# Two float32 products in place of split float16 ones, in an attention chain with a written-out order

## The chip, the cores and the metric

The kernel runs on one core of a Trainium2 chip. The metric is the device time of one execution in microseconds; lower is better.

## The reference

Three layers run one after the other: a gated delta-rule attention over 768 steps for 4 batches and 8 heads of 48 columns, a layer of 8 experts of which each token takes one, and a feed-forward layer.

```python
k_n = k / (np.linalg.norm(k, axis=-1, keepdims=True) + 1e-06)
state = np.zeros((B, H, D, D), dtype=np.float32)          # B, H, D = 4, 8, 48
for t in range(S):                                        # S = 768
    kt, vt, bt = (k_n[:, :, t], v[:, :, t], beta[:, :, t, None])
    y[:, :, t] = np.einsum('bhd,bhde->bhe', q[:, :, t], state)
    v_old = np.einsum('bhde,bhd->bhe', state, kt)
    state = state + bt[:, :, :, None] * np.einsum('bhd,bhe->bhde', kt, vt - v_old)
...
logits = x @ w_gate; expert_idx = np.argmax(logits, axis=1)
out[mask] = gate_w[mask, None] * (np.maximum(xe @ w1[e], 0.0) @ w2[e])   # for each expert e
...
h = x @ w_in
return ((h * (1.0 / (1.0 + np.exp(-h)))) @ w_out).astype(np.float32)
```

## The kernel before, in words

The 768 steps are cut into 6 chunks of 128. A *group* is one chunk of one batch with all 8 heads, 24 groups in all; two batches make a *pair*, 12 pairs, and the state of a batch goes from one chunk to the next, which is two pairs or four groups later. For a group the kernel does:

- load k, q and v (`lk`, `lq`, `lv`, DMAs on SP's queue), normalise k and q (`kn`, `nrm...`), and split each into a float16 high and low part (`knh`, `knl` into the tile `TMk`; `qh`, `ql`), transpose them by DMA (`trk`, `trq`), and copy rows of the transposed k to `KX` by three DMAs (`kx`);
- the Gram matrices: L is K K' under a mask, P is K Q' under a mask. `mm0` to `mm3` write a bank of PSUM each, `mt0` to `mt3` multiply it by the mask on VectorE, `mh...` takes the float16 high part on ScalarE, `ml...` the low part on GpSimd. A bank holds two heads, each with L and P side by side;
- invert the triangular matrix: its 16x16 diagonal blocks go through a scratch in DRAM (`scr`, `lm`), are inverted on VectorE and GpSimd with one block on each partition (`l0` to `lo`), and come back (`st`, `tv`) as the tile `TV`; three levels of products double the blocks (`xm`, `xe`, `Tm`, `Te`, `Vm`, `Ve` with 16, 32 and 64);
- the chain: `rm` multiplies the state (two float16 parts in `Ss`) by K, `re` and `rh` form the right side, `z0m` and `z0h` apply the inverse, `em` and `ee` form the residual with both parts of L, `zm` corrects. The result Z is split in two (`zh` on ScalarE, `zl` on VectorE). `sm` adds K'Z to the state (three float16 products for each head), `se`, `sh` and `sl` store it and its two parts in partitions 0 to 47 of `Ss`, and `sd` copies them to partitions 64 to 111, so that one product takes both parts of k or q. `ym` forms P Z (three products for each head) and adds the state's part; `ye` scales it;
- the router's part: transpose (`rt`), logits in float32 (`rl`, line 900), and the places of the tokens.

The class `Plan` writes the order of all these steps once for every engine and for SP's queue, by a table of steps with durations and needs (`GROUP`, `PAIR`), a table of which buffers are held from which step to which (`GHELD`, `PHELD`), and a table of shifts (`LATER`); on the chip each engine then works off its own queue in that order. The experts and the feed-forward part follow; no step of theirs is touched.

Lines of the profile: 529 is `mm`, 533 `mt`, 538 `mh`, 543 `ml`; 722 is the state's product in `rm` and `ym`; 773 `zh`, 777 `zl`; 784 to 786 `sm`; 798 `sl`; 801 `sd`; 807 to 809 `ym`; 552 `scr`, 557 `tv`, 473 `kx`, 645 the larger products of the block inversion.

Of the kernel before, what the change touches and what calls it, by code (L numbers as in the profile page):

```python
# [24 lines left out]
ISC = 1.0 / SC  # L25
# [3 lines left out]
class Plan:  # L29
# [17 lines left out]

    GHELD = """k lk / sqk kn; q lq / sqq ql; s2 sqk / sqr; s2 sqq / sqq; s2 vq / vq; kn kn / knl; TTk trk / rm mm0 mm1 mm2 mm3; TTq trq / ym mm0 mm1 mm2 mm3; KX kx / mm0 mm1 mm2 mm3;
        t mt0 / ml0; t mt1 / ml1; t mt2 / ml2; t mt3 / ml3; Mh mh0 mh1 mh2 mh3 / ym; Ml ml0 ml1 ml2 ml3 / ym; TV tv / zm; Rh rh / zm; Z0h z0h / zm; Z0s zs / em; Zh zh / sm ym;
        Zl zl / sm ym; xT rc / rl; pm mm0 / mt0; pm mm1 / mt1; pm mm2 / mt2; pm mm3 / mt3; pi xm16 / xe16; pi Tm16 / Te16; pi Vm16 / Ve16; pi xm32 / xe32; pi Tm32 / Te32;  # L50
        pi Vm32 / Ve32; pi xm64 / xe64; pi Vm64 / Ve64; pc rm / re; pc em / ee; pc sm / se; pc ym / ye; pz z0m / z0h; pz zm / zl; pr rt / rc; pr rl / rg"""
# [7 lines left out]
    LAND = dict(lk=3.4, lq=2.8, lv=2.7, trk=2.8, trq=2.7, kx=2.2, scr=2., lm=5., st=5., tv=4., rs=4.)  # L59
    START = dict(P=0.5, A=1, V=0.7, G=0.7, D=1.75)  # L60
    EARLY, LOOK = 14.40, 0.00
    LATER = dict(
        l42=226, ql=9, ee=-190, l22=198, vp=14, rt=61, Vm16=98, zl=-42, z0m=-172, ml1=4, l40=10, Te32=6, xm16=-111, z0h=-6, mm2=75, vr=-7, rb1=160,
        rb3=-152, mh2=-84, xe16=-29, nrm2=210, ym=13, xm32=-49, mm3=10, Tm32=-146, rp=-89, l21=6, em=-44, mt2=-48, mt0=-4, xe32=-7, trk=6, Vm64=-19,
        knl=-120, bl0=-42, l8c=-30, Ve64=-12, zt1=-2, nrs=-81, sh=-3, sm=-90, zx64=59, se=-20, l8b=2, l43=-4, b1=29, b3=-52, zs2=10, lo=-8, l0p=-34,
        nrm1=15, sd=51, zs0=20, kn=-25, zxo=10, l23=-124, zt7=16, nrm0=-18, Te16=30, l0=7, rb=2, lm=-6, vu1=-23, zk0=-30, b2=-14, nrm7=6)
    SLOW = 1.4

    def __init__(self, chunks, pairs, bufs, held, scratch, setup):
# [36 lines left out]
        for s in ("knh", "knl"):  # L106
            for r in ("sm", "trk"):
                after(s, r, held)
# [151 lines left out]
class Attention:  # L260
# [6 lines left out]
    BUFS = dict(k=3, q=3, v=3, ss=2, r0=1, r1=1, w=5, rn=2, s2=1, kn=1, TTk=6, TTq=8, KX=2, t=3, Mh=8, Ml=8, Lm=2, Ln=1, Tl=2, pr=1, Xl=1, TVl=1, TV=3,  # L267
                Rh=2, Z0h=2, Z0s=2, Zh=2, Zl=2, ysc=2, m1=2, m2=2, vsc=6)
    TMK, NSCR = 8, 2
# [22 lines left out]
    def constants(self):  # L292
# [4 lines left out]
        self.TMk = [cp.tile([128, 8, 128], F16, name=f"TMk{i}") for i in range(self.TMK)]  # L297
        self.TMq = cp.tile([128, 8, 128], F16, name="TMq")
# [13 lines left out]
    def setup(self):  # L312
# [18 lines left out]
        z = self.wk.tile([128, 1, 1028], F16, tag="Ml", name="zeros16", bufs=self.BUFS["Ml"])  # L331
# [4 lines left out]
        for i, t in enumerate(self.Ss):  # L336
            add(f"zs{i}", "G", 0.4, [], [(i, "sh")], zero(t))
# [77 lines left out]
    def front(self, pi, g, c, b, a, pr):  # L415
# [3 lines left out]
        TMk = self.TMk[g % self.TMK]  # L419
# [34 lines left out]
        def kn():  # L454
            st["kn"] = self.sb([H, D], F32, "kn")
            nc.gpsimd.tensor_tensor(out=st["kn"], in0=st["k"], in1=self.bc(pr["rn"][:, a, 0:8], D), op=ALU.mult)
# [7 lines left out]
        def knh():  # L464
            nc.scalar.activation(out=self.part(TMk, False), in_=st["kn"], func=AF.Copy)

        def knl():
            nc.gpsimd.tensor_tensor(out=self.part(TMk, True), in0=st["kn"], in1=self.part(TMk, False), op=ALU.subtract)
# [44 lines left out]
    def bank(self, i):  # L513

        return slice(2 * i, 2 * i + 2)

    def grams(self, pi, g, c, b, a, pr):
# [3 lines left out]
        out = []  # L521
        for i in range(4):
            def mm(i=i):
                mp = st["mp", i] = self.pm.tile([128, 2, 256], F32, tag="pm", name="mp")
# [10 lines left out]
            def mh(i=i):  # L535
                if "Mh" not in st:
                    st["Mh"] = self.sb([H, 256], F16, "Mh")
# [170 lines left out]
    def chain(self, pi, g, c, b, a, pr):  # L708
# [91 lines left out]
        def sd():  # L800
            nc.vector.tensor_copy(Ss[64:112], Ss[0:48])
# [561 lines left out]
```

## Time and profile before

| | us |
|---|---|
| median of 3 runs (lowest, highest) | 1137.92 (1135.22, 1139.65) |
| the profiled execution's own time | 1134.98 |
| its span, first to last instruction | 1133.2 |

| engine | busy in the span | share |
|---|---|---|
| TensorE (PE) | 932.6 us | 82% |
| VectorE (DVE) | 671.9 us | 59% |
| ScalarE (ACT) | 539.0 us | 48% |
| GpSimd (POOL) | 368.3 us | 33% |

The shares are means over two different parts. In the first 440 us, the attention with the router, the engines share the work and none is full; after that TensorE works nearly without a break. The page's clock row (PEclk) gives the granted TensorE clock in tenths of the full one: 6 to 9 in the first part, 9 in the second. A busy time of an engine is the time covered by its instructions, and an instruction that stands behind something after it began counts as busy.

### The profile page before, as it was taken

How to read it: one execution, taken by the hardware profiler on the slowest of the kernel's cores; microseconds unless marked ns; L12 is line 12 of the kernel's file. 1: busy time of each engine (PE TensorE's matmuls, PEld its weight loads, DVE VectorE, ACT ScalarE, POOL GpSimd, SP SyncE). 2: the span in 40 equal slices, each digit the busy share in tenths (PEclk: the TensorE clock that was granted, in tenths of full speed). 3: DMA queues.
4: the chain of work that ended last, by engine and by line, in shares of the span. 5: the costliest groups of instructions: out<-in, count | busy, mean ns of one | idle time of the engine just before them, and what ended most of it. 6: DMA issues, size and time to landing. Idle time of an engine off the chain costs nothing. (4 is left out here: it accounts for less than half of the span.)

```text
span 1133.2 us, 21329 instructions
## 1 busy us (share of the span) xinstructions
PE 932.6 (82%) x8404; PEld 843.4 (74%) x8405; DVE 671.9 (59%) x1371; ACT 539.0 (48%) x1094; POOL 368.3 (33%) x353
## 2 busy tenths in 40 slices
PE   0437766676777874589999999999999999999995
PEld 0436666575666763579899999899999999999995
DVE  5797888988798843544444469974333343433332
ACT  4547767676767673434333344643233233323321
POOL 5866555756566312553233320001001010100101
PEclk9657767868678796699999999999999999999998
DMA  8885766857677523643344444520000000000000
GB/s 227 178 168 105 164 142 124 186 106 151 132 149 114 102 54 104 188 133 115 114 136 136 136 150 130 154 70 28 1 1 28 1 29 1 15 15 1 28 1 31
DMA packets 223667, 108.96 MB, mean 96 GB/s; under 512 B 164296, under 2 KB 210120, under 8 KB 223560
## 3 DMA queue, kind: packets, MB, share of 16 engines
q1 hardware_dynamic: 219208, 97.37, 36.6%
q0 software_dynamic: 4352, 10.16, 2.9%
q8 instruction: 68, 1.11, 0.5%
q14 instruction: 39, 0.32, 0.2%
HBM read 71.34 MB, written 16.50 MB: 78 GB/s over the span
## 5 line engine op out<-in xcount | busy, mean ns | idle before, releaser
L1099 PE MATMUL po<-w,g 128*128 128x384 f32 x1152 | 218.4, 338 | 0.0
L1099 PE MATMUL pf<-yb,w 128*128 128x512 f32 x864 | 216.6, 395 | 1.0 <-ACT yb L1174 0.5
L1099 PEld LDWEIGHTS po<-w,g 128*128 128x128 f32 x1152 | 204.7, 188 | 9.0 <-ACT g L1189 0.4
L1099 PEld LDWEIGHTS pf<-yb,w 128*128 128x128 f32 x864 | 161.2, 188 | 31.4 <-DVE yb L1175 0.9
L1216 POOL DMA_INDIRECT out_dram<-ob,idsi x24 | 25.0, 1043 | 440.4 <-DVE ob L1215 434.9
L1187 DVE TENSOR_TENSOR sg<-pf,sg 128x512 f32<-128x512 f32 x96 | 66.2, 690 | 171.8 <-ACT sg L1186 171.7
L1186 ACT ACTIVATE sg<-pf 128x512 f32<-128x512 f32 x96 | 57.4, 598 | 194.1 <-PE pf L1099 193.4
L543 POOL TENSOR_TENSOR Ml<-t,Mh 128x512 f16<-128x512 f32 x96 | 113.4, 1194 | 59.6 <-ACT Mh L538 58.2
L1099 PE MATMUL py<-h,w 128*128 128x432 f32 x576 | 127.7, 362 | 5.3 <-ACT yT L1139 3.4
L1099 PE MATMUL ph<-xT,w 128*128 128x432 f32 x576 | 125.7, 363 | 1.0 <-DVE xT L1071 1.0
L1099 PEld LDWEIGHTS py<-h,w 128*128 128x128 f32 x576 | 106.1, 188 | 13.5 <-DVE h L1122 4.4
L1099 PEld LDWEIGHTS ph<-xT,w 128*128 128x128 f32 x576 | 110.1, 191 | 6.5 <-DVE xT L1071 1.3
L529 PEld LDWEIGHTS <-KX 112*128 112x128 f16 x768 | 67.7, 127 | 52.8 <-issue 32.0
L529 PE MATMUL mp<-TTk,KX 112*128 112x128 f16 x384 | 67.7, 273 | 47.6 <-DVE t L533 29.2
L1190 DVE TENSOR_TENSOR g<-sg,g 128x512 fp32r<-128x512 f32 x96 | 66.3, 691 | 55.1 <-PE po L1099 41.8
L1189 ACT ACTIVATE g<-sg 128x512 fp32r<-128x512 f32 x96 | 60.6, 631 | 62.6 <-DVE sg L1187 62.5
L1045 DVE TENSOR_TENSOR w<-raw,w 128x768 fp32r<-128x768 f32 (+1 forms) x56 | 60.6, 1093 | 30.4 <-ACT w L1044 30.1
L538 ACT ACTIVATE Mh<-t 128x512 f16<-128x512 f32 x96 | 59.4, 625 | 39.6 <-DVE t L533 38.9
L533 DVE TENSOR_TENSOR t<-mp,c 128x512 f32<-128x512 f32 x96 | 64.8, 682 | 17.1 <-PE mp L529 15.4
L1121 ACT ACTIVATE h<-ph 128x432 fp32r<-128x432 f32 x64 | 33.6, 524 | 76.6 <-PE ph L1099 74.8
L1044 ACT ACTIVATE w<-raw 128x768 fp32r<-128x768 f32 (+1 forms) x56 | 51.6, 934 | 33.7 <-DMA raw<-in_moe_w_dram 33.6
L529 PE MATMUL mp<-TTq,KX 112*128 112x128 f16 x384 | 67.5, 276 | 0.0
(189 smaller groups left out, 1750.8 us busy)
## 6 DMA issues: line engine op xcount, KB each, us to landing
TV<-scr SPq DMA_DIRECT2D x24, 512.0 KB, 4.5
raw<-in_moe_w_dram SPq DMA_DIRECT2D x24, 512.0 KB, 4.3
raw<-in_moe_w_dram SPq DMA_DIRECT2D x32, 384.0 KB, 4.0
KX<-TTk SPq DMA_DIRECT2D x72, 96.0 KB, 3.3
raw<-in_moe_w_in_dram SPq DMA_DIRECT2D x12, 512.0 KB, 4.9
raw<-in_moe_w_out_dram SPq DMA_DIRECT2D x16, 384.0 KB, 3.1
xd<-x SPq DMA_DIRECT2D x12, 392.0 KB
k<-in_k_dram SPq DMA_DIRECT2D x24, 192.0 KB, 2.8
```

What stands on the lines that cost most here:

```text
L529: nc.tensor.matmul(mp[:, j, o:o + 128], KX[0:112, x, u], st[t][0:112, u], start=x == 0, stop=x == 1)
L533: nc.vector.tensor_tensor(out=t, in0=st["mp", i], in1=self.con.mask.to_broadcast([128, 2, 256]), op=ALU.mult)
L538: nc.scalar.activation(out=st["Mh"][:, self.bank(i)], in_=st["t", i], func=AF.Copy)
L543: nc.gpsimd.tensor_tensor(out=st["Ml"][:, self.bank(i)], in0=st["t", i], in1=st["Mh"][:, self.bank(i)], op=ALU.subtract)
L1044: nc.scalar.activation(out=h, in_=x, func=AF.Copy)
L1045: (nc.gpsimd if slow else nc.vector).tensor_tensor(out=l, in0=x, in1=h, op=ALU.subtract)
L1099: self.nc.tensor.matmul(out, a, b, start=first and i == 0, stop=last and i == n - 1)
L1121: nc.scalar.activation(out=h[:, 0, 0:W], in_=ph[:, 0:W], func=AF.Relu)
L1186: nc.scalar.activation(out=gf, in_=ph, func=AF.Sigmoid)
L1187: nc.vector.tensor_tensor(out=gf, in0=ph, in1=gf, op=ALU.mult)
L1189: nc.scalar.activation(out=g[:, 0], in_=gf, func=AF.Copy)
L1190: nc.vector.tensor_tensor(out=g[:, 1], in0=gf, in1=g[:, 0], op=ALU.subtract)
```

## The change

The products P Z and K'Z become float32: Z is kept as one float32 tile, P as the masked float32 tile `Pt`, and K as the normalised float32 tile `KN` (8 fixed ones instead of one in turn). So `zl` goes, and only L has a high and a low part: `mh` and `ml` are two for a group, not four. A Gram bank now holds four heads of L (`mm0`, `mm1`, which need only `kx`) or four heads of P (`mm2`, `mm3`, which also need the transposed q). The state's copy `sd` becomes a DMA on SP's queue. The buffers change: `Mh` and `Ml` from 8 of 256 columns a head to 5 of 128, `Pt` 6, `TMk` from 8 to 3. The tables of durations, buffers and shifts of `Plan` change with it, and so the written order on all engines.

```diff
-        mt0 V .6 mm0; ... mh0 A .52 mt0; mh1 A .52 mt1; mh2 A .52 mt2; mh3 A .52 mt3; ml0 G 1.11 mh0; ...
+        mt0 V .6 mm0; ... mh0 A .55 mt0; mh1 A .55 mt1; ml0 G 1.11 mh0; ml1 G 1.11 mh1;
...
-    EARLY, LOOK = 14.40, 0.00
+    EARLY, LOOK = 19.26, 0.00
...
-        l42=226, ql=9, ee=-190, l22=198, vp=14, rt=61, Vm16=98, zl=-42, z0m=-172, ml1=4, ...
+        l42=193, vp=14, Vm16=98, zl=-42, ml1=17, l40=-105, Te32=6, xm16=-26, z0h=-6, ...
-    SLOW = 1.4
+    SLOW = 1.2
...
-                for j, u in enumerate(range(H)[self.bank(i)]):
-                    for o, t in ((0, "TTk"), (128, "TTq")):
-                        for x in range(2):
-                            nc.tensor.matmul(mp[:, j, o:o + 128], KX[0:112, x, u], st[t][0:112, u], start=x == 0, stop=x == 1)
+                for j, u in enumerate(range(H)[s]):
+                    for x in range(2):
+                        nc.tensor.matmul(mp[:, j], KX[0:112, x, u], st[t][0:112, u], start=x == 0, stop=x == 1)
...
-            st["Zh"] = self.sb([H, D], F16, "Zh")
+            st["Zh"] = self.sb([H, D], F32, "Zh")
             nc.scalar.activation(out=st["Zh"], in_=st["zq"], func=AF.Copy, scale=ISC)
-
-        def zl():
-            st["Zl"] = self.sb([H, D], F16, "Zl")
-            nc.vector.scalar_tensor_tensor(out=st["Zl"], in0=st["zq"], scalar=ISC, in1=st["Zh"], op0=ALU.mult, op1=ALU.subtract)
...
             for u in range(H):
-                h, l = (TMk[:, u, r:r + 48] for r in (0, 64))
-                nc.tensor.matmul(sp[:, u], h, Zh[:, u], start=True, stop=False)
-                nc.tensor.matmul(sp[:, u], l, Zh[:, u], start=False, stop=False)
-                nc.tensor.matmul(sp[:, u], h, Zl[:, u], start=False, stop=True)
+                nc.tensor.matmul(sp[:, u], KN[:, u], st["Zh"][:, u], start=True, stop=True)
...
         def sd():
-            nc.vector.tensor_copy(Ss[64:112], Ss[0:48])
+            nc.sync.dma_start(Ss[64:112], Ss[0:48])
...
             for u in range(H):
-                h, l = st["Mh"][:, u, 128:256], st["Ml"][:, u, 128:256]
-                nc.tensor.matmul(yp[:, u], h, st["Zl"][:, u], start=True, stop=False)
-                nc.tensor.matmul(yp[:, u], h, st["Zh"][:, u], start=False, stop=False)
-                nc.tensor.matmul(yp[:, u], l, st["Zh"][:, u], start=False, stop=c == 0)
+                nc.tensor.matmul(yp[:, u], st["Pt"][:, u], st["Zh"][:, u], start=True, stop=c == 0)
                 if c > 0:
                     state(yp[:, u], ("TTq", u), False)
```

On TensorE, at a head of P Z (`pc` is the bank of PSUM, `Ss` the state, `TTq` the transposed q), before:

```order
L807 LDWEIGHTS Mh
L807 MATMUL pc<-Zl,Mh 128x48
L808 LDWEIGHTS Mh
L808 MATMUL pc<-Zh,Mh 128x48
L809 LDWEIGHTS Ml
L809 MATMUL pc<-Zh,Ml 128x48
L722 LDWEIGHTS TTq
L722 MATMUL pc<-Ss_128,TTq 128x48
L722 LDWEIGHTS TTq
L722 MATMUL pc<-Ss_128,TTq 128x48
```

and now, with two heads:

```order
L811 MATMUL pc<-Zh,Pt 128x48
L736 LDWEIGHTS TTq
L736 MATMUL pc<-Ss_131,TTq 128x48
L736 LDWEIGHTS TTq
L736 MATMUL pc<-Ss_131,TTq 128x48
L811 MATMUL pc<-Zh,Pt 128x48
```

The three pairs of weights and product are one float32 product, whose weights have no row of their own here; the state's two products stay between them.

On VectorE, in the middle of the attention part, from one right side (`v`) through the state's low part (`Ss<-Sm`) to the state's copy, before:

```order
L777 SCALAR_TENSOR_TENSOR Zl<-pz,Zh 128x384
L732 SCALAR_TENSOR_TENSOR v<-v,vsc,pc 128x384
L437 TENSOR_REDUCE ss<-s_4397 128x8
L792 SCALAR_TENSOR_TENSOR Sm_125<-pc,vsc,Sm_125 48x384
L509 TENSOR_SCALAR ysc<-w,vsc 128x2
L798 SCALAR_TENSOR_TENSOR Ss_129<-Sm_125,vsc,Ss_129 48x384
L533 TENSOR_TENSOR t<-mp,c_71 128x512 x2
L751 TENSOR_TENSOR Z0s<-Z0h,sign 128x384
L533 TENSOR_TENSOR t<-mp,c_71 128x512
L581 TENSOR_SCALAR Ln<-Lm 128x256
L801 COPY Ss_129<-Ss_129 48x768
```

and now:

```order
L746 SCALAR_TENSOR_TENSOR v<-v,vsc,pc 128x384
L542 TENSOR_TENSOR Lt<-mp,c_71 128x512 x2
L765 TENSOR_TENSOR Z0s<-Z0h,sign 128x384
L797 SCALAR_TENSOR_TENSOR Sm_127<-pc,vsc,Sm_127 48x384
L776 SCALAR_TENSOR_TENSOR Rh<-pc,v 128x384
L803 SCALAR_TENSOR_TENSOR Ss_131<-Sm_127,vsc,Ss_131 48x384
L542 TENSOR_TENSOR Pt<-mp,c_71 128x512
L689 TENSOR_TENSOR X_119<-lv,c_71 128x32x16
L746 SCALAR_TENSOR_TENSOR v<-v,vsc,pc 128x384
```

The low part of Z and the copy have no row any more; the masked copies write `Lt` twice, then `Pt`.

On SP's queue, where the first chunk's states are stored, before:

```order
L638 DMA scr_104<-TVl 128x16x16 x2
L477 DMA_TRANSPOSE TTq<-TMq 128x8x128
L428 DMA k<-in_k_dram 128x384
L428 DMA v<-in_v_dram 128x384 x2
L473 DMA KX_114<-TTk 48x1024 x3
L552 DMA scrM<-Mh 64x8x64 x2
L477 DMA_TRANSPOSE TTq<-TMq 128x8x128
L557 DMA TV<-scr_104 128x8x256
```

and now:

```order
L434 DMA v<-in_v_dram 128x384
L806 DMA Ss_131<-Ss_131 48x768
L434 DMA v<-in_v_dram 128x384
L566 DMA scrM<-Mh 64x8x64 x2
L434 DMA k<-in_k_dram 128x384
L482 DMA_TRANSPOSE TTk<-TMk_105 128x8x128
L434 DMA q<-in_q_dram 128x384
L482 DMA_TRANSPOSE TTq<-TMq 128x8x128
L478 DMA KX_117<-TTk 48x1024 x3
L806 DMA Ss_132<-Ss_132 48x768
```

The state's copy (`Ss`) stands among the loads, the scratch write and the transposes of other groups.

## Rows read from the trace of the kernel before

**Rows 1.** Busy time by stretch (us, instructions), then granted clock, DMA share, GB/s

```profile
core 0: us, PE busy (x) PEld busy (x) DVE busy (x) ACT busy (x) POOL busy (x), PEclk, DMA share, GB/s
0.00:60.00 60.00, 16.03 (x134) 13.95 (x135) 39.87 (x97) 31.86 (x76) 40.41 (x63) 0.81 0.87 204
60.00:360.00 300.00, 205.20 (x3686) 182.04 (x3687) 257.44 (x597) 204.01 (x478) 188.87 (x184) 0.74 0.72 141
360.00:440.00 80.00, 63.43 (x1316) 55.58 (x1314) 48.07 (x132) 52.05 (x120) 20.28 (x18) 0.81 0.33 72
440.00:1133.00 693.00, 647.97 (x3269) 591.82 (x3269) 326.52 (x549) 251.04 (x422) 118.74 (x89) 0.97 0.23 70
```

**Rows 2.** Groups of DVE, 0 to 440 us: busy us, mean ns | idle before

```profile
L533 DVE TENSOR_TENSOR t<-mp,c 128x512 f32<-128x512 f32 x96 | 64.8, 682 | 17.1 <-PE mp L529 15.4 <-POOL Ml L543 0.8 <-POOL v L446 0.6
L798 DVE SCALAR_TENSOR_TENSOR Ss<-Sm,vsc,Ss 48x384 f16<-48x384 f32 x20 | 22.0, 1098 | 0.8 <-ACT Ss L795 0.8
...
L801 DVE COPY Ss<-Ss 48x768 f16<-48x768 f16 x20 | 18.8, 942 | 0.6
...
L777 DVE SCALAR_TENSOR_TENSOR Zl<-pz,Zh 128x384 f16<-128x384 f32 x24 | 13.2, 550 | 7.1 <-ACT Zh L773 7.0
...
L501 DVE TENSOR_TENSOR r<-r,r 128x18 f32<-128x18 f32 x12 | 7.2, 604 | 0.2
```

**Rows 3.** Single lines of DVE: shortest, median and longest ns

```profile
L801 DVE COPY Ss<-Ss x20: 353/386/3153, 114.9 to 408.7; 48x768 f16<-48x768 f16 x20
...
L798 DVE SCALAR_TENSOR_TENSOR Ss<-Sm,vsc,Ss x20: 598/604/3656, 113.5 to 407.6; 48x384 f16<-48x384 f32 x20
...
L501 DVE TENSOR_TENSOR r<-r,r x12: 156/178/1950, 15.6 to 309.6; 128x18 f32<-128x18 f32 x12
```

**Rows 4.** Timeline near 246 us, DVE and POOL: start us, duration us

```profile
246.28 1.52 POOL L645 TENSOR_TENSOR pr<-Tl,Xl 128x512 f32<-128x512 f32 x1
246.60 2.52 DVE L801 COPY Ss<-Ss 48x768 f16<-48x768 f16 x1
...
247.75 1.16 POOL L543 TENSOR_TENSOR Ml<-t,Mh 128x512 f16<-128x512 f32 x1
```

**Rows 5.** The page's costliest groups: low and high parts of the Gram banks

```profile
L543 POOL TENSOR_TENSOR Ml<-t,Mh 128x512 f16<-128x512 f32 x96 | 113.4, 1194 | 59.6 <-ACT Mh L538 58.2
...
L538 ACT ACTIVATE Mh<-t 128x512 f16<-128x512 f32 x96 | 59.4, 625 | 39.6 <-DVE t L533 38.9
```

**Rows 6.** Groups of PE, 60 to 360 us: the first product of P Z

```profile
L807 PE MATMUL pc<-Zl,Mh 128*128 128x48 f16 x128 | 19.2, 199 | 1.8 <-DVE v L732 1.4 <-DVE Sm L792 0.4
```

**Rows 7.** Timeline of PE, four places: P Z twice, the logits twice

```profile
239.82 0.21 PE L807 MATMUL pc<-Zl,Mh 128*128 128x48 f16 x1
239.86 0.21 PE L808 MATMUL pc<-Zh,Mh 128*128 128x48 f16 x1
...
434.80 0.18 PE L808 MATMUL pc<-Zh,Mh 128*128 128x48 f16 x1
434.83 0.18 PE L809 MATMUL pc<-Zh,Ml 128*128 128x48 f16 x1
...
245.42 0.81 PE L900 MATMUL ps<-wg,xT 128*128 128x8 f32 x6
246.10 0.35 PE L688 MATMUL lv<-X,TV 128*128 128x32 f16 x8
...
264.01 1.45 PE L900 MATMUL ps<-wg,xT 128*128 128x8 f32 x6 [0.83 <-ACT xT L895]
265.31 0.48 PE L767 MATMUL pz<-Z0h,c 128*128 128x384 f16 x1
```

**Rows 8.** DMA issues: count, KB each, median us to landing

```profile
KX<-TTk SPq DMA_DIRECT2D x72, 96.0 KB, 3.3
```

**Rows 9.** Waits of SP's queue, 0 to 436 us: total us, times, longest

```profile
SPq L557 <- PE pz L769: 23.6, 4, 8.5
```

**Rows 10.** Waits of all engines, 60 to 420 us: total us, times, longest

```profile
PE pc L786 <- DVE Zl L777: 9.4, 9, 2.8
```

More of the change, by code (lines that the diff above doesn't have):

```diff
@@ L106, in __init__ @@
         for s in ("knh", "knl"):
-            for r in ("sm", "trk"):
-                after(s, r, held)
+            after(s, "trk", held)
+        for s in ("knl", "sm"):
+            after("kn", s, normed)
         for s in ("rm", "ym"):
@@ L297, in constants @@
         self.TMk = [cp.tile([128, 8, 128], F16, name=f"TMk{i}") for i in range(self.TMK)]
+        self.KN = [cp.tile([128, 8, 48], F32, name=f"KN{i}") for i in range(self.NKN)]
         self.TMq = cp.tile([128, 8, 128], F16, name="TMq")
@@ L324, in setup @@
             add(n, "G", 0.15, [], u, zero(t.rearrange("p u (r c) -> p (u r) c", r=2)[:, :, 48:64]))
+        for i, t in enumerate(self.Ss):
+            add(f"zs{i}", "G", 0.4, [], [(i, "sh")], zero(t))
         for i, t in enumerate(self.KX):
@@ L464, in knh @@
         def knh():
-            nc.scalar.activation(out=self.part(TMk, False), in_=st["kn"], func=AF.Copy)
+            nc.scalar.activation(out=self.part(TMk, False), in_=KN, func=AF.Copy)
         def knl():
-            nc.gpsimd.tensor_tensor(out=self.part(TMk, True), in0=st["kn"], in1=self.part(TMk, False), op=ALU.subtract)
+            nc.gpsimd.tensor_tensor(out=self.part(TMk, True), in0=KN, in1=self.part(TMk, False), op=ALU.subtract)
         def kx():
@@ L511, in norms, with four @@
         return [("nrs", nrs), *self.steps("nrm", nrm), ("ysc", ysc)]
-    def bank(self, i):
-        return slice(2 * i, 2 * i + 2)
+    def four(self, i):
+        return slice(4 * i, 4 * i + 4)
     def grams(self, pi, g, c, b, a, pr):
@@ L536, in mh, with ml @@
+            out += [(f"mm{i}", mm), (f"mt{i}", mt)]
+        for i in range(2):
+            s = self.four(i)
+            def mh(s=s):
                 if "Mh" not in st:
-                    st["Mh"] = self.sb([H, 256], F16, "Mh")
-                nc.scalar.activation(out=st["Mh"][:, self.bank(i)], in_=st["t", i], func=AF.Copy)
-            def ml(i=i):
+                    st["Mh"] = self.sb([H, 128], F16, "Mh")
+                nc.scalar.activation(out=st["Mh"][:, s], in_=st["Lt"][:, s], func=AF.Copy)
+            def ml(s=s):
@@ L541, in ml @@
                 if "Ml" not in st:
-                    st["Ml"] = self.sb([H, 256], F16, "Ml")
-                nc.gpsimd.tensor_tensor(out=st["Ml"][:, self.bank(i)], in0=st["t", i], in1=st["Mh"][:, self.bank(i)], op=ALU.subtract)
-            out += [(f"mm{i}", mm), (f"mt{i}", mt), (f"mh{i}", mh), (f"ml{i}", ml)]
+                    st["Ml"] = self.sb([H, 128], F16, "Ml")
+                nc.gpsimd.tensor_tensor(out=st["Ml"][:, s], in0=st["Lt"][:, s], in1=st["Mh"][:, s], op=ALU.subtract)
+            out += [(f"mh{i}", mh), (f"ml{i}", ml)]
@@ L667, in xm @@
                 for u in range(H):
-                    nc.tensor.matmul(xp[:, u], st["Mh"][:, u, 0:128], Ta[:, u], start=m != 16 or u == 0, stop=m != 16)
+                    nc.tensor.matmul(xp[:, u], st["Mh"][:, u], Ta[:, u], start=m != 16 or u == 0, stop=m != 16)
                 if m == 16:
```

86 lines of the change are left out of this document (43 added, 43 removed).

## The prediction

> **What bounds the kernel now.** I read the table of stretches first [rows 1]. The program is two programs in a row: the attention part with the router until about 440 us, and the experts and the feed-forward part after it. The diff touches only the first, so its 440 us are what can change. In the long middle of it, 60 to 360 us, no engine is full: VectorE (DVE) is busy 257.4 of 300 us, TensorE (PE) 205.2, ScalarE (ACT) 204.0, GpSimd (POOL) 188.9, and the DMA engines have a busy share of 0.72. TensorE's granted clock is 0.74 there, so it changes between its two levels of 1.2 and 2.4 GHz. The engine nearest to full is DVE, at 86%; the missing 14% are waits on other engines in queues of fixed order. That is why I treat DVE as what sets the pace, with a rate of 300/257.4 = 1.17 us of time for each us of the busiest engine.
>
> Then I read what DVE spends its time on [rows 2], and the shortest, median and longest time of its forms [rows 3]. The copy of the state (L801) has a median of 386 ns and a mean of 942; the low part of the state (L798) 604 and 1098; a tiny 128x18 sum (L501) 178 and 604. In the order of time one sees why [rows 4]: the copy that began at 246.60 ended at 249.12, while POOL ran two tensor operations back to back from 246.28 to 248.91. DVE's busy time thus holds time in which it only stood behind POOL.
>
> **The change part by part.**
>
> *VectorE.* The low part of Z (L777, 24 x 550 ns = 13.2 us) and the copy of the state (L801, 18.8 us) go: 32.0 us [rows 2]. The masked copies of the Gram banks (L533) stay 96 of 128x512. The waits behind POOL shrink too. In L798 they are 20 x (1098 - 604) = 9.9 us, in L501 12 x (604 - 178) = 5.1 [rows 2, 3]. POOL loses half of its 113.4 us of low parts of the Gram matrices [rows 5], 56.7 of the 40.4 + 188.9 + 20.3 = 249.6 us it is busy up to 440 us [rows 1], so 23%. I take 23% of these 15 us, 3 us; the bounds are nothing and all 15, since I cannot tell which POOL instruction caught which DVE one. Sum for DVE: -35 us of 345.4 [rows 1], three quarters of it in the middle stretch (257.4/345.4), -26: it falls from 257 to 231 us.
>
> The Trainium skill (SBUF — State Buffer, "SBUF: two separate sides") says that DVE and GpSimd share one pair of ports as an exclusive lock, held for a whole instruction, against a DVE operation in a two-port mode or with two SBUF inputs. The long copy agrees [rows 4]; by that rule the copy's 11 us of waiting go whole (they are in the 18.8 already), and what is left falls with POOL's share, as above.
>
> *ScalarE and GpSimd.* Half of the high parts (L538, 48 x 625 ns = 30 us) and half of the low parts (L543, 48 x 1194 ns = 57 us) go [rows 5]. Neither engine is the fullest, so I give their time nothing by itself; it shortens the queues in which others' work stands.
>
> *TensorE.* Here the change costs. P Z took 24 float16 products of 48 columns for a group (8 heads x 3), each with its own weights; they follow each other every 40 ns where the clock is low and every 25 to 30 where it is high [rows 7]. Now it is 8 float32 products. The trace has one float32 product with weights of 128x128 already, the router's logits (L900): three products show as six instructions, and the next work begins 0.68 us after them at the high level (245.42 to 246.10) and 1.30 us after at the low one (264.01 to 265.31) [rows 7]. That is 0.113 and 0.217 us for an instruction. Eight products are 16 such: 1.8 us at the high level, 3.5 at the low one, against 24 x 0.025 = 0.6 and 24 x 0.040 = 0.96 before. They move 48 columns where the logits move 8; if that does not hide behind the loading of weights it adds at most two float16 steps of 40 ns to each, 16 x 0.297 = 4.8 us. So P Z costs +1.2 to +3.8 us for a group. With a mean clock of 0.74, about half of the time is at each level, so 16 x 0.167 = 2.7 against 0.8: +1.9.
>
> K'Z goes from 24 products to 8 in float32 with weights of 48 columns. No row shows those weights. Below, they keep the float16 pace: 16 x 0.040 = 0.64 for 24 x 0.040 = 0.96, a gain of 0.3 us. Above, they cost as much as the logits: 2.7 for 0.8, +1.9. I take +0.5, nearer to the float16 end because the weights are three eighths as wide. L807, the first of P Z's products, stands 128 times in the middle stretch, 8 for a group: 16 groups [rows 6]. TensorE then has 205 + 16 x (1.9 + 0.5) = 243 us there; the bounds are 205 + 16 x 0.9 = 219 and 205 + 16 x 5.7 = 296.
>
> The Trainium skill (TensorE: Matmul & The Clock Gate, "Weight-path perf modes — Fast Weight Load (FWL) and DoubleRow") speaks against the change: quick loading of weights is on for 128 columns of a type that is not FP32, so float32 weights lose it. The trace agrees as far as it goes: 40 ns for a float16 step, 217 for a float32 one at the same level [rows 7]. By the page's P / 1.2 ns, 107 ns for a load of 128 columns, P Z would be 16 x 0.107 = 1.7 us, an estimate that the rows outdo.
>
> *The DMA.* The second copy of the state becomes 20 transfers on SP's queue, each behind the low part of the state (L798) of its batch, so each can hold up what follows it there. In the row of the new order, loads of v, k and q and the transposes stand behind it; those feed groups that come later. The nearest row is the copy of K' rows (KX, also 48 partitions): 3.3 us to landing [rows 8]. The copy is wanted one chunk later, four groups on; at 300/16 = 19 us a group for the middle that is over 50 us. So its landing is hidden. If the queue is late, the cost is that of the waits below, in the third rival.
>
> *The order of the Gram banks.* At the start the banks of L of groups 0 and 1 now come before any bank of P. The scratch write of L of the first pair waits for two masked copies and two high parts for a group, not four: 2 x 682 + 2 x 625 ns = 2.6 us for a group, 5 for the pair [rows 2, 5]. POOL, busy 40.4 of the first 60 us, has less in front too [rows 1]. I take -6 us for the start, between 0 and -12. In the last stretch, 360 to 440 us, PE is busy 63.4 of 80 us and DVE only 48.1 [rows 1], so there the longer P Z counts: the groups end one behind the other, and of +1.9 - 0.55 us for each of the last few about 3 us stay, between 0 and +8.
>
> **Sum.** The fullest engine of the middle goes from DVE's 257 us to PE's 243 (DVE 231): 14 us less, at 1.17 us each -16. With -6 at the start and +3 at the end: -19 us. The profiled execution, from which all durations are, took 1134.98 us (span 1133.2), so 1116 by its own time; the median of the runs shown is 1137.92, 3 us more, and so 1119 us.
>
> **The rivals.**
>
> *VectorE keeps the pace (faster still).* If TensorE's work packs tighter and the high clock holds, PE has 219 us, DVE all of the relief behind POOL: 257 - (32 + 15) x 0.75 = 222. Then 222 x 1.17 = 259, -41 in the middle, -6 at the start: 1091 us. For it: PE waits 9.4 us in K'Z for the low part of Z alone, and that goes [rows 10]. Against it: DVE and PE would then be equally full, and queues of fixed order wait for both.
>
> *TensorE becomes the bound (slower).* The float32 products run at the low level, and the columns do not hide: P Z 4.8 - 0.96 = +3.8 us, K'Z +0.7, together +4.5. PE has 205 + 72 = 277 us, at 1.17 that is 324: +24 in the middle, +5 at the end, 1167 us. It decides from 52/16 = 3.3 us for a group upwards, where PE reaches the 257 us that DVE has now. For it: the granted clock of 0.74, and that half of the logits shown ran at the low level [rows 1, 7]. Against it: the logits' step includes their own moving columns, and PE now has 95 idle us in the stretch to take work into.
>
> *The queue of SP holds the pace (no change).* SP's queue already stands for 23.6 us, in four places, with the load of the inverses (L557) behind a product of TensorE [rows 9]. Twenty more transfers, each stuck behind DVE for a us or two, are 20 to 40 us of the queue; the loads behind come later by as much, and the relief of the engines becomes idle time: 1138, within 6. Against it: the scratch write gets half of its wait removed, and the loads run one or more groups ahead.
>
> **How the numbers follow.** A difference of 0.5%, 5.7 us, is about what a measurement of this kernel can tell from none. The forecast has a chance of 0.47, VectorE's pace 0.22, TensorE as the bound 0.17, SP's queue 0.14. Faster: nearly all of the first, all of the second and a third of the last: 0.70. Slower: nearly all of the third rival but one, a little of the last: 0.16. Same: 0.14. For 8 in 10 the range goes from the fast rival, 1091, to 1148, which leaves out the dear half of the slow one. The forecast's own range is 1103 to 1132.
>
> **What would show it.** The stretch up to the experts is about 20 us shorter and the rest as long as before. DVE has no L777 and no state copy, and forms such as L798 have a mean nearer to their median of 604 ns. POOL's low parts are 48. P Z takes 2.7 us of PE for a group and K'Z about 1.3; PE, not DVE, is the fullest engine of the middle. The state's DMA lands in some 3 us and nobody waits for it. I am wrong if P Z takes over 4 us, if SP's queue waits for the state's low part by tens of us, or if the groups follow each other as slowly as now though every engine has less to do.

## The result and the profile after

The changed kernel takes 1147.08 us (median of 20 runs, 1137.72 to 1156.27) beside 1137.99 us for the kernel before on the same chip: the ratio is 1.0073, 95% interval [1.0053, 1.0093]. It is slower by 6 to 11 us, where I had forecast 19 us faster.

The table of stretches of the changed kernel answers to [rows 1]. The second boundary is now 453 us, where the last logits leave TensorE (439.8 before):

```profile
0.00:60.00 60.00, 17.04 (x134) 14.59 (x135) 41.15 (x103) 28.10 (x66) 34.88 (x53) 1.00 0.85 197
60.00:360.00 300.00, 243.66 (x3582) 223.83 (x3583) 218.50 (x570) 189.70 (x452) 138.34 (x142) 0.78 0.76 146
360.00:453.00 93.00, 77.38 (x1071) 69.18 (x1068) 35.88 (x106) 46.22 (x107) 18.95 (x16) 0.71 0.31 68
453.00:1146.00 693.00, 648.22 (x3269) 593.23 (x3269) 327.04 (x550) 251.48 (x423) 118.19 (x89) 0.97 0.23 70
```

The experts need 693 us as before, so the attention part lost all of it: 13 us in the profiled executions. In its middle TensorE (first column) is busy 243.66 us, the forecast's 243; VectorE (third) 218.50, less than the forecast's 231. No engine is as full as VectorE was (257.44), and yet the stretch up to the experts is longer. The same 300 us hold 17 groups of P Z (272 instructions, 16 a group) where they held 16 before [rows 6]:

```profile
L811 PE MATMUL pc<-Zh,Pt 128*128 128x48 f32 x272 | 52.2, 333 | 5.5 <-DVE v L746 5.4
```

So the middle is not where the changed kernel falls behind. Behind 360 us it needs 93 us for the last 7 groups of P Z, where the kernel before needed 80 for 8; TensorE is busy 77.38 us there instead of 63.43.

Where it went is seen from the copy of a group's output Y, the last step of each group's chain. These are the answers on that line, of the kernel before and of the changed one (shortest, median, longest ns; start of the first and the last of 24):

```profile
L817 ACT ACTIVATE x<-pc,ysc x24: 560/580/582, 109.8 to 436.0; 128x384 f32<-128x384 f32 x24
```

```profile
L819 ACT ACTIVATE x<-pc,ysc x24: 557/580/582, 95.2 to 449.4; 128x384 f32<-128x384 f32 x24
```

The first group is done 14.6 us sooner, the other 23 take 354.2 us instead of 326.2, 28.0 more. The loss isn't spread evenly over them. These are the 15th copies, of the kernel before and of the changed one (start, duration in us):

```profile
343.64 0.58 ACT L817 ACTIVATE x<-pc,ysc 128x384 f32<-128x384 f32 x1
```

```profile
326.27 0.58 ACT L819 ACTIVATE x<-pc,ysc 128x384 f32<-128x384 f32 x1
```

Up to there the changed kernel is still 17.4 us ahead. Its last nine copies take 123.1 us instead of 92.4, 30.8 more.

The groups of VectorE, GpSimd and ScalarE, 0 to 453 us, answer to [rows 2, 5]:

```profile
L542 DVE TENSOR_TENSOR Pt<-mp,c 128x512 f32<-128x512 f32 x48 | 32.7, 681 | 11.0 <-PE mp L536 8.4 <-PE pc L811 2.3
L542 DVE TENSOR_TENSOR Lt<-mp,c 128x512 f32<-128x512 f32 x48 | 32.2, 683 | 11.4 <-PE mp L536 7.9 <-POOL Ml L557 3.2
L803 DVE SCALAR_TENSOR_TENSOR Ss<-Sm,vsc,Ss 48x384 f16<-48x384 f32 x20 | 19.3, 964 | 2.0 <-ACT Ss L800 1.8
L746 DVE SCALAR_TENSOR_TENSOR v<-v,vsc,pc 128x384 f32<-128x384 f32 x20 | 12.2, 611 | 14.2 <-PE pc L736 14.2
L506 DVE TENSOR_TENSOR r<-r,r 128x18 f32<-128x18 f32 x12 | 3.9, 326 | 0.2
...
L557 POOL TENSOR_TENSOR Ml<-Lt,Mh 128x512 f16<-128x512 f32 x48 | 55.7, 1178 | 39.8 <-ACT Mh L552 39.6
...
L552 ACT ACTIVATE Mh<-Lt 128x512 f16<-128x512 f32 x48 | 28.5, 621 | 6.0 <-PE pc L771 2.9 <-DVE Lt L542 2.7
```

The halved counts are there. What is new stands behind the last bar of a line: VectorE waits 14.2 us for TensorE before the right side (L746). Before, it was 1.8 on that step:

```profile
L732 DVE SCALAR_TENSOR_TENSOR v<-v,vsc,pc 128x384 f32<-128x384 f32 x20 | 12.1, 606 | 1.9 <-PE pc L722 1.8
```

The groups of TensorE, 0 to 460 us, and its timeline at two places answer to [rows 6, 7]:

```profile
L811 PE MATMUL pc<-Zh,Pt 128*128 128x48 f32 x384 | 75.5, 335 | 5.5 <-DVE v L746 5.4
L791 PE MATMUL pc<-Zh,KN 128*48 128x48 f32 x320 | 22.8, 237 | 3.9 <-ACT Zh L786 3.4
```

```profile
257.88 0.40 PE L811 MATMUL pc<-Zh,Pt 128*128 128x48 f32 x2
258.12 0.21 PE L736 MATMUL pc<-Ss,TTq 112*128 112x48 f16 x2
258.18 0.40 PE L811 MATMUL pc<-Zh,Pt 128*128 128x48 f32 x2
...
301.44 0.66 PE L811 MATMUL pc<-Zh,Pt 128*128 128x48 f32 x2 [3.35 <-DVE v L746]
301.90 0.28 PE L736 MATMUL pc<-Ss,TTq 112*128 112x48 f16 x2
302.00 0.64 PE L811 MATMUL pc<-Zh,Pt 128*128 128x48 f32 x2
302.45 0.28 PE L736 MATMUL pc<-Ss,TTq 112*128 112x48 f16 x2
```

A float32 product is two instructions (x384 for 192 products). A head of P Z with its two state products takes 0.30 us at the high clock and 0.56 at the low one; the float32 product alone is 0.24 (257.88 to 258.12) and 0.46 (301.44 to 301.90): 1.9 and 3.7 us for eight heads, as the logits had foretold (1.8 and 3.5).

The state's copy as a DMA, with the scratch loads and K' rows beside it (KB, us to landing), and SP's waits behind it, answer to [rows 8, 9]:

```profile
TV<-scr SPq DMA_DIRECT2D x24, 512.0 KB, 7.5
KX<-TTk SPq DMA_DIRECT2D x72, 96.0 KB, 2.4
Ss<-Ss SPq DMA_DIRECT2D x20, 72.0 KB, 2.4
```

```profile
SPq L806 <- DVE Ss L803: 24.3, 7, 11.7
```

The copy lands in 2.4 us, but SP's queue stands 24.3 us for it, "tens of us", one of the signs that I had named as against me. The queue shows a second thing: the two TV loads of a pair now go out back to back, and the transpose behind them takes 7.02 us to issue, the next one 1.25:

```profile
290.86 1.73 SPq L571 DMA_DIRECT2D TV<-scr  x2
292.68 0.76 SPq L434 DMA_DIRECT2D k<-in_k_dram  x1
293.56 0.36 SPq L586 DMA_DIRECT2D Lm<-scrM  x1
294.01 7.02 SPq L482 DMA_TRANSPOSE TTk<-TMk  x1
301.12 1.25 SPq L482 DMA_TRANSPOSE TTq<-TMq  x1
```

So three suspects: TensorE's queue (theory P), the loads in SP's queue (S), the state's DMA (D). I followed the waits back from the last logits, each to what released it; this chain is worked out from the trace and is no view of the profile. In 60 to 360 us VectorE held 146 us of it before and TensorE 35; now TensorE holds some 100 and VectorE 42. DMAs hold some 80 us where they held 34, so the chain spoke for S too. Behind 360 us TensorE holds 55 of the 93 us, where it held 22 of 80. That spoke for P and settled nothing.

### The profile page after: what moved, and what is told of

It is laid out like the page before. It is cut to its first block, busy times and chain, and to the rows that moved or that the text cites. A ratio compares the mean times of both kernels' runs of the same rounds, so it can differ in the third digit from the quotient of the medians.

```text
span 1146.3 us, 20488 instructions
## 1 busy us (share of the span) xinstructions
PE 986.3 (86%) x8052; PEld 900.8 (79%) x8053; DVE 622.6 (54%) x1327; ACT 515.5 (45%) x1046; POOL 310.4 (27%) x300
## 5 line engine op out<-in xcount | busy, mean ns | idle before, releaser
L536 PEld LDWEIGHTS <-KX 112*128 112x128 f16 x768 | 66.3, 126 | 30.1 <-DMA KX<-TTk 12.6
L811 PE MATMUL pc<-Zh,Pt 128*128 128x48 f32 x384 | 75.5, 335 | 5.5 <-DVE v L746 5.4
L811 PEld LDWEIGHTS pc<-Zh,Pt 128*128 128x128 f32 x384 | 71.0, 240 | 6.3 <-DVE v L746 6.0
L557 POOL TENSOR_TENSOR Ml<-Lt,Mh 128x512 f16<-128x512 f32 x48 | 55.7, 1178 | 39.8 <-ACT Mh L552 39.6
L1124 DVE SCALAR_TENSOR_TENSOR h<-ph,h 128x432 fp32r<-128x432 f32 x64 | 38.5, 601 | 50.1 <-ACT h L1123 49.4
L682 PE MATMUL lv<-TV,Mh 128*128 128x64 f16 x576 | 36.1, 218 | 26.2 <-DMA TV<-scr 22.2
```

The lines of the kernel that those rows point to most:

```text
L536: nc.tensor.matmul(mp[:, j], KX[0:112, x, u], st[t][0:112, u], start=x == 0, stop=x == 1)
L557: nc.gpsimd.tensor_tensor(out=st["Ml"][:, s], in0=st["Lt"][:, s], in1=st["Mh"][:, s], op=ALU.subtract)
L682: nc.tensor.matmul(xp[:, u], st["Mh"][:, u], Ta[:, u], start=m != 16 or u == 0, stop=m != 16)
L811: nc.tensor.matmul(yp[:, u], st["Pt"][:, u], st["Zh"][:, u], start=True, stop=c == 0)
L1124: nc.vector.scalar_tensor_tensor(out=h[:, 1, 0:W], in0=ph[:, 0:W], scalar=0.0, in1=h[:, 0, 0:W], op0=ALU.max, op1=ALU.subtract)
```

## The experiments

Ratios are to the kernel before, timed beside each version, with 95% intervals; a difference between two of them is turned into time with 1138 us. The changed kernel was timed once, with its 1.0073, and was not timed again beside the versions of it.

**The three suspects.** e1 takes the length of the float32 products away, with all writers and the order kept:

```
+    def top(self, t): return t.bitcast(mybir.dt.bfloat16)[:, :, 1::2]
-    matmul(sp[:, u], KN[:, u], st["Zh"][:, u], ...)
+    matmul(sp[:, u], self.top(KN)[:, u], self.top(st["Zh"])[:, u], ...)
     (P Z, L811, likewise)
```

> The changed kernel in its own order, but P Z and K'Z read only the upper 16 bits of each float32 operand as bfloat16 (the operands are still written in float32; the low parts of both products are left out). The float32 products were 75.5 us on TensorE for P Z alone with the state's steps; at float16's 40 ns a product the 24 groups should be about 35 us shorter on TensorE. Theory P (TensorE's in-order queue paces the pairs: it holds 99 of the 300 us of the chain of waits in 60 to 360 us, VectorE 42): the last router copy comes 10 to 20 us sooner than at 453 us and the time is 1127 to 1138. Theory S (the two state-independent 512 KB loads that stand back to back in SP's queue make k and the transposes late): the stalls stay, 1144 to 1149. Theory D (the state's copy as a DMA holds SP's queue): 1144 to 1149.

1124.91 us, ratio 0.9882 [0.9839, 0.9925]: 22 us faster than the changed kernel and faster than the kernel before. Of e1, P Z's group of TensorE, and the stretch up to the last logits:

```profile
L811 PE MATMUL pc<-Zh,Pt 128*128 128x48 bf16 x192 | 18.6, 195 | 5.9 <-DVE v L746 5.8
```

```profile
0.00:428.00 428.00, 284.49 (x4431) 251.75 (x4432) 292.61 (x777) 264.25 (x623) 189.66 (x211) 0.75 0.72 144
```

and the same stretch of the changed kernel:

```profile
0.00:453.00 453.00, 338.08 (x4783) 307.61 (x4784) 295.54 (x777) 264.02 (x624) 192.18 (x211) 0.79 0.68 137
```

TensorE has 53.6 us less, the others the same within 3 us. Theory P holds: 21.7/53.6 = 0.40 us of time for each us of TensorE (0.30 to 0.51 by the intervals of the two ratios), though it was busy only 81% of the middle. This is a mean over the whole part. At the 15th copy of Y, e1 is 7.1 us ahead of the changed kernel, at the last one 24.3, so most of it comes in the last nine groups:

```profile
319.15 0.56 ACT L819 ACTIVATE x<-pc,ysc 128x384 f32<-128x384 f32 x1
```

```profile
L819 ACT ACTIVATE x<-pc,ysc x24: 557/572/582, 94.9 to 425.1; 128x384 f32<-128x384 f32 x24
```

e2 moves the loads:

```
 SP:  ... scr1 tv0 tv1 lk lm trk trq ...   ->   ... scr1 lk tv0 lm trk tv1 trq ...
```

> The changed kernel with one edit on SP's queue: from the fourth pair on, the second of a pair's two TV loads is issued behind the next Lm load and transpose instead of right behind the first TV load, and the k load stands ahead of both. Theory S: the transpose behind the loads is issued in 1.3 us again instead of 4 to 7, k no longer holds ScalarE (17.5 us in all), and with some 3 us a pair back over 7 pairs the time is 1126 to 1136. Theory P: the waits move to TensorE's queue, at most 3 us come back, 1143 to 1148. Theory D: no change, 1145 to 1149.

1150.02 us, 1.0094 [1.0058, 1.0130], as the changed kernel. Between 60 and 420 us ScalarE's wait for k falls from 17.5 to 2.4 us; TensorE's wait for TV is 26.2 instead of 22.2. The transposes between the loads still took 3.6 to 4.4 us, so SP's queue was relieved only in part. What was relieved of the once-a-pair stall that I had thought most telling was worth nothing; the rest was not tried.

e3 puts the copy back:

```
-            nc.sync.dma_start(Ss[64:112], Ss[0:48])
+            nc.vector.tensor_copy(Ss[64:112], Ss[0:48])
```

> The changed kernel with the state's second copy made by VectorE again at the same place of the same order (20 copies, 20 fewer DMAs of 72 KB). Theory D: SP's queue no longer waits for sl (24.3 us in all, longest 11.7), the loads behind it go out earlier, 1130 to 1140. Theories P and S: VectorE has room (218 us of 300), so little either way, 1144 to 1150.

1152.94 us, 1.0109 [1.0066, 1.0151]. Theory D falls in its strong form: without the DMA the time does not come down. But the copy gives VectorE 13.0 us of work again:

```profile
L806 DVE COPY Ss<-Ss 48x768 f16<-48x768 f16 x20 | 13.0, 650 | 0.6
```

By the prices of VectorE below that costs some 4 to 6 us, which can hide a gain of the same size. So e3 shows that the DMA is no worse than the copy, not that the 24.3 us in SP's queue cost nothing.

e4 adds TensorE's time to the kernel before:

```
+                for i in range(7):
-                nc.tensor.matmul(yp[:, u], h, st["Zl"][:, u], start=True, stop=False)
+                    nc.tensor.matmul(yp[:, u], h, st["Zl"][:, u], start=True, stop=i < 6)
```

> The kernel before with six more copies of one 128x48 float16 product per head in P Z (each overwritten, so the output is the same): by 25 to 40 ns each 1.2 to 1.9 us more on TensorE's queue in each of 24 groups, 29 to 46 us in all, and nothing else changed. Theory P: TensorE's queue is close to the pace even there, and a third to a half of that shows, 1148 to 1160. If VectorE alone paces the kernel before and TensorE's time is free, 1137 to 1141, and then the float32 products alone cannot be the cause.

1151.64 us, 1.0111 [1.0073, 1.0149]: 12.6 us by the ratio. Up to the last logits TensorE is busy 23.0 us more than before (307.66; 284.7 by [rows 1]), VectorE 342.58, as before:

```profile
0.00:448.00 448.00, 307.66 (x6287) 274.64 (x6288) 342.58 (x821) 288.43 (x671) 249.54 (x264) 0.79 0.69 135
```

That is 0.55 us (0.36 to 0.74 by the interval) for each us of an engine that was not the fullest. The busy time rose by less than the 29 to 46 us of products that were expected; TensorE's granted clock is 0.79 in this stretch and was 0.76 in the kernel before.

**Which product.** e5 is e1 for P Z alone, e6 for K'Z alone.

> The changed kernel in its own order with only P Z reduced to the upper 16 bits of its operands (bfloat16; P Z's low parts are left out), K'Z in float32 as it is. With both reduced, TensorE was busy 51 us less up to 450 us and the time fell by some 23 us, 0.45 us per us. P Z has about 40 of the 51 us. Theory P by total (each us on TensorE's queue counts alike): 18 us, so 1128 to 1133. If K'Z is the costly one since the state waits for it: 1137 to 1145.

> The counterpart: only K'Z reduced to the upper 16 bits (its low parts are left out), P Z in float32. Theory P by total: some 10 us of TensorE, 4 to 6 us of time, 1141 to 1146. If K'Z is the costly one: 1128 to 1135, and e5 shows little.

e5: 1130.99 us, 0.9938 [0.9914, 0.9962]. e6: 1150.33, 1.0113 [1.0080, 1.0147]. P Z carries it: TensorE has 47.6 us less up to the last logits of e5 and the time is 15 us less, 0.32. e6 is a miss for theory P by total: TensorE has 16.7 us less and the time is 4.6 us more, 0.1 to 9 by the intervals. Taken away alone, K'Z gains nothing; from e5 to e1, where P Z is already short, it goes with 6 us, good to 6. So not every us of TensorE has the same price.

e8 keeps more bits at a middle length:

```
-        self.KN = [cp.tile([128, 8, 48], F32, ...
+        self.KN = [cp.tile([128, 8, 48], F32R, ...
     (Zh and Pt likewise; the Lt tiles stay F32)
```

> The changed kernel with KN, P and Z stored as float32r and both products taken in float32r instead of float32, the same count of instructions in the program and the same order; what float32r rounds away of the operands is left out. No trace here shows a 128x48 product in float32r. If it takes as long as float16's (bounds: 40 ns at the full clock from the row of float16, 0.2 us from float32): theory P gives 1124 to 1130. If it takes as long as float32's: 1146 to 1150.

1132.44 us, 0.9952 [0.9927, 0.9977], faster than both kernels. A product is one instruction, and P Z's share lies between:

```profile
L811 PE MATMUL pc<-Zh,Pt 128*128 128x48 f32 x192 | 44.6, 315 | 6.9 <-DVE v L746 6.8
```

P Z's busy time of 18.6 us goes with 1125 (e1) and 1131 us (e5), 44.6 with 1132, 75.5 with 1147. TensorE has 303.3 us up to the last logits of e8, 34.8 less than in the changed kernel, and the time is 0.0121 x 1138 = 13.8 us less: 0.40 again (0.29 to 0.50).

**Length or place.** P Z stands ahead of a chain step that waits for ScalarE and VectorE (E's product of the other group). e7 puts it behind; e9 puts its second half there; e12 is e9 in float32r:

```
 PE, e7:        zm0 .. sm0 z0m1 ym0 em1 ..   ->   .. z0m1 em1 ym0 ..
 PE, e9, e12:   zm0 .. sm0 z0m1 ym0 em1 ..   ->   .. z0m1 ym0[0:4] em1 ym0[4:8] ..
```

> The changed kernel, all products in float32, with one edit of the order on TensorE: P Z of each group stands behind the next instruction group of TensorE instead of ahead of it (behind E's product or z0 of the other group, behind V16 of the next pair), so that 2.3 to 4.4 us of P Z no longer hold up a step of the chain. TensorE's total is the same. Theory P by position (the long run of P Z is the cost because chain steps stand behind it): half or more of P Z's share comes back, 1134 to 1142. Theory P by total (any work on TensorE's queue costs the same wherever it stands): 1145 to 1150.

> The changed kernel in float32 with P Z of each group cut in two: heads 0 to 3 where P Z stands, heads 4 to 7 behind the next instruction group of TensorE (behind E's product of the other group, or V16 of the next pair). The products are the same. P Z took 2.45 us a group at the full clock and 4.49 at half; in the kernel before 1.09 and 1.66. Theory W (P Z lies in the wait for z0 to pass ScalarE and VectorE, a wait of 1 to 2 us, and only what stands over is paid): halves of 1.2 to 2.2 us fit such a wait, and half or more of the 15 to 18 us that P Z's length costs comes back, 1131 to 1140. Theory P by total: 1145 to 1150. As e7, where P Z behind that step cost 8 us more: 1152 to 1160.

> The float32r version (P Z 1.53 us a group at the full clock, 2.65 at half) with P Z cut in two halves placed as in the float32 kernel of the same call. Theory W: the halves of 0.8 to 1.3 us fit the wait, and some 4 to 7 us of the 7 that P Z in bfloat16 gave on top come back, 1125 to 1129. Theory P by total: 1130 to 1135. If the second half disturbs the step behind it: above 1138.

e7: 1157.43 us, 1.0177 [1.0146, 1.0207]; e9: 1156.99, 1.0148 [1.0122, 1.0174]; e12: 1134.68, 0.9957 [0.9937, 0.9978]. Theory W falls: halves gained nothing in either form. Theory P by total misses too, since e7 and e9 take 12 and 9 us more than the changed kernel with the same products: the place counts as well, and later is worse. P Z already stood at the better of these places, and what could be won was its length (e1, e5, e8).

**Order and buffers.** e10 tells the planner of e8's shorter products (two numbers: ym 2.30 to 1.30, sm .90 to .70). e11 gives e8 ten KN and six Mh and Ml in the same order. e16 is e11 with e2's order of loads.

> The float32r version with the planner told of it: 1.30 us for P Z instead of 2.30 and 0.70 for K'Z instead of 0.90, so that it writes another order. If the order written for the longer products is part of the loss: 1118 to 1128. If the order's costs do not matter: 1128 to 1137, as the float32r version (1132). Above 1140 would say that any other order is worse.

> The float32r version in the same order with 10 instead of 8 KN buffers and 6 instead of 5 for Mh and Ml, so that GpSimd's wait for K'Z of four pairs ago (17.3 us in 60 to 360 us) goes. Theory P: that wait is only the reflection of TensorE's pace, 1129 to 1136. Theory B (the buffers close the loop: a pair follows when KN comes free): the pairs follow 1 us sooner, 1118 to 1127.

> The float32r version with the larger KN, Mh and Ml of e11 and the TV loads apart as in e2. Theory S in a weaker form (the TV loads matter once TensorE is relieved; k's DMA holds 47 us of the chain of e11): 1122 to 1128. If they still do not matter: 1128 to 1134.

e10: 1174.69 us, 1.0292 [1.0268, 1.0315], 39 us slower than e8 with the same instructions. Two better estimates gave a far worse order. That suggests that the planner's numbers are tuned together; no run shows why. It also shows that an order alone can be worth more than the whole change. e11: 1131.15, 0.9910 [0.9880, 0.9940]. GpSimd's wait for KN (17.3 us in the middle of e8) is gone, but its wait for ScalarE's high part of k grows from 18.3 to 38.0, ScalarE's own for k stays at 20.2, and the time is 5 us less by the ratios, good to 4, and 1 us less by the medians. e16: 1133.65, 0.9980 [0.9954, 1.0007]: no gain from the loads with TensorE relieved either.

**The price of VectorE.** e13, e14 and e15 make two of four mask products of each group twice, in the kernel before, the changed one and e8:

```
+                for _ in range(i // 2 + 1):
                     nc.vector.tensor_tensor(out=..., in0=st["mp", i], in1=..., op=ALU.mult)
```

> The kernel before with two of the four mask products of each group made twice (48 more VectorE instructions of about 0.6 us, some 29 us more on VectorE, 19 of them in 60 to 360 us; the output is the same). By the prediction's rule (the middle stretch lasts 1.17 times VectorE's work, 257 of 300 us) the time rises by 22 us or more, 1160 to 1172. If an engine's added microsecond counts as TensorE's did in e4 (0.34 to 0.47): 10 to 14 us, 1148 to 1155. If VectorE has slack: 1137 to 1143.

> The changed kernel with the two mask products of P of each group made twice (48 more VectorE instructions of 0.68 us, 32 us; the output is the same). If TensorE alone paces the changed kernel, VectorE (218 of 300 us) has room: 1146 to 1152. If each engine's microsecond counts in part whichever is the fullest: 8 to 15 us more, 1155 to 1165.

> The float32r version (1132 us, VectorE 216 and TensorE 224 of 300 us) with the same 48 more VectorE instructions, 32 us. If VectorE's relief is what the change gains, putting it back costs as much: by 0.4 us per us some 13 us, 1142 to 1148. If VectorE's relief gains nothing: 1130 to 1136, and the gain of the float32r version over the kernel before has its cause elsewhere (the earlier start).

e13: 1153.44 us, 1.0140 [1.0099, 1.0182]; e14: 1159.57, 1.0182 [1.0138, 1.0227]; e15: 1140.87, 1.0035 [1.0009, 1.0060]. The masked copies of e13, 0 to 460 us, beside the 64.8 us of [rows 2]:

```profile
L534 DVE TENSOR_TENSOR t<-mp,c 128x512 f32<-128x512 f32 x144 | 97.9, 686 | 17.1 <-PE mp L529 13.9 <-POOL Ml L544 0.8 <-POOL v L446 0.6
```

and P's of e14, beside 32.7 in the changed kernel:

```profile
L543 DVE TENSOR_TENSOR Pt<-mp,c 128x512 f32<-128x512 f32 x96 | 65.7, 686 | 11.1 <-PE mp L536 7.1 <-PE pc L812 2.3
```

33 us more each. They cost 15.9 us in the kernel before, 12.4 in the changed one and 9.4 in e8 (the latter two by differences of ratios taken at different times, each good to 4 to 6 us): 0.48, 0.38 and 0.28 us for each us of added work. By the prediction's rule e13 would have been 1160 or more.

These are not yet prices like TensorE's above, which go by an engine's whole busy time. The stretches up to the last logits of e13, e14, e8 and e15 are:

```profile
0.00:460.00 460.00, 295.45 (x5135) 258.26 (x5136) 367.28 (x870) 289.21 (x672) 250.72 (x264) 0.73 0.64 131
```

```profile
0.00:465.00 465.00, 340.36 (x4783) 309.22 (x4784) 320.02 (x828) 265.26 (x625) 190.68 (x211) 0.78 0.67 133
```

```profile
0.00:436.00 436.00, 303.31 (x4431) 270.98 (x4432) 291.00 (x777) 264.00 (x624) 191.53 (x211) 0.71 0.71 142
```

```profile
0.00:444.00 444.00, 310.38 (x4431) 277.83 (x4432) 319.23 (x825) 264.82 (x623) 190.46 (x211) 0.76 0.70 139
```

VectorE's busy time rises by 21.9 us in e13 (from 345.4), 24.5 in e14 (from 295.5) and 28.2 in e15 (from 291.0), since its other instructions take less. By busy time its price is 0.73, 0.51 and 0.33. In e13 TensorE is also busy 10.8 us longer, at a granted clock of 0.73 instead of 0.76, so part of the 15.9 us may be TensorE's.

## Why the prediction was wrong

**The step that failed** is the one that turned work into time: "The fullest engine of the middle goes from DVE's 257 us to PE's 243 (DVE 231): 14 us less, at 1.17 us each -16." It priced the fullest engine at 1.17 us for each us and every other at nothing until it is fuller. Measured as a mean over the part, TensorE costs 0.40 (e1, e8) to 0.55 (e4) while VectorE is the fuller and while it is not, and VectorE 0.28 to 0.48 for each us of added work (0.33 to 0.73 by its busy time). No engine was a bound: the queues have a fixed order and wait for each other, and a us put on either engine shows in part.

**A second term failed**, the one of the end: "+1.9 - 0.55 us for each of the last few about 3 us stay, between 0 and +8". I gave the longer P Z a full price there, but for a few groups alone. By the stretches behind 360 us the end takes 13 us more for one group less, by the copies of Y 30.8 us more for the last nine. Start and middle together were to gain 22 us; by the 15th copy of Y they gained 17.4. By the work still open there is no lead: at 360 us TensorE has 77.4 of its 338.1 us in front, 23%, and had 63.4 of 284.7, 22%. So the middle gained less than forecast, by how much depends on the measure, and by either measure the end took more than my bound.

**The sum with these prices.** Up to the last logits VectorE lost 345.4 - 295.5 = 50 us and TensorE gained 338.1 - 284.7 = 53: at about 0.4 each they cancel. The runs split it so: everything but the length of the products is worth 0.0118 x 1138 = 13 us to the good (e1 against before, TensorE at 284.5 us in both), the length 22 to the bad, and 8 are left. The 13 us, good to 5, lie at the lower end of what VectorE's relief would give by the prices above (14 to 24 at 0.28 to 0.48, more by its busy time). They are no proof of those prices: the whole new order is in them as well. What VectorE, GpSimd, ScalarE, the buffers, the order and the earlier start have in it was not tried apart.

**TensorE's sizes were near**: the float32 product as from the logits, and 53 us in 24 groups, 2.2 a group, for my 2.4. That the middle shows 243 us exactly is partly luck, since it holds 17 groups and not the 16 that I counted. K'Z, 22.8 us in 20 groups or 1.1 each, is near the 1.3 that I took, and its length alone did not matter (e6).

**VectorE's size was low**: 50 us less for my 35. The low part of Z and the copy are 32 of it, as forecast. The other 18 are in instructions that stayed and took less, for my 3 and beyond my bound of 15, which counted the waits of two lines alone. Those shrank in L803 from 9.9 to 20 x (964 - 610) = 7.1 us and in L506 from 5.1 to 12 x (326 - 178) = 1.8, 6 in all; these are the shortest, median and longest ns:

```profile
L803 DVE SCALAR_TENSOR_TENSOR Ss<-Sm,vsc,Ss x20: 599/610/3433, 97.1 to 407.6; 48x384 f16<-48x384 f32 x20
...
L506 DVE TENSOR_TENSOR r<-r,r x12: 166/178/1082, 12.9 to 306.5; 128x18 f32<-128x18 f32 x12
```

The Trainium skill (SBUF — State Buffer, "SBUF: two separate sides") says that a GpSimd operation that reads SBUF and a VectorE operation with two SBUF inputs take one shared pair of ports as an exclusive lock. The trace agrees in direction: with 57 us less GpSimd work, these two lines wait 8.9 us instead of 15.0.

**The start** gained 14.6 us to the first copy of Y, not 6, beyond my bound of 12. It is not all gain: e1's first copy comes at 94.9, its last at 425.1, so its 24 groups take 330.2 us, 4 more than before with less work on three engines. A group that starts sooner meets the same queues. In e1, too, the end is the slow part: its last nine copies take 106 us where the kernel before took 92.4, with TensorE's work as before. So something in the change other than the length makes the end longer, or leaves more of the work for it; which part of it stays open.

**The rivals.** SP's queue had the sign that I named, and no run that relieved it became faster (e2, e3, e16); each relieved it in part or at a price. TensorE as the bound had the right engine and side. Its condition, "from 52/16 = 3.3 us for a group upwards", was wrong: +2.2 us a group were enough, since there is no point from which it decides. With a price of 0.4 on both engines my own sizes give 0.4 x (38 - 26) - 6 + 3 = +2 us, no change; that is still not the 8 measured.

## What to carry to other kernels

Where no engine is full (86% at most here) and the queues have a fixed order, don't take the fullest engine for the clock: price a us on each engine apart, and measure that price by repeating a harmless instruction (e4, e13) before trading work from one engine to another. Look at the end of a chain by itself: a mean over the part hid that the changed kernel was ahead up to the 15th of 24 copies of Y. Here the length of the float32 products cost 22 us on TensorE's queue and everything else in the change gave 13; float32r at 0.6 of that length was enough to turn the change from 0.7% slower to 0.5% faster. A long wait in a queue is a suspect and no more: 24 us in SP's queue went away for no gain that could be seen, and 17 for KN for 5 that are barely clear of the noise.

## What the runs showed that I had not expected

- A float32r product of 128x48 is one instruction and a float32 one two: with the two state products a head takes 0.18 us instead of 0.30 at the high clock (timeline of e8):

```profile
283.81 0.27 PE L811 MATMUL pc<-Zh,Pt 128*128 128x48 f32 x1
283.93 0.22 PE L736 MATMUL pc<-Ss,TTq 112*128 112x48 f16 x2
283.99 0.27 PE L811 MATMUL pc<-Zh,Pt 128*128 128x48 f32 x1
```

- Operands read as every second 16-bit element (e1) cost no more: L811's mean is 195 ns, that of float16 products in the kernel before 199 [rows 6].
- A transpose issued behind two 512 KB loads held SP's queue for up to 7.02 us; the next one took 1.25.
